# The last twelve row tiles of w2: summed straight into the result's bank, in five transfers, behind the fold

## The chip, the cores and the metric

One NeuronCore of one Trainium2 chip runs the whole program. The metric is device microseconds of that core. Before the change the median is 772.49 us over three timed runs, 772.41 to 772.53 us. The profile is one more execution of the same program, taken by the hardware profiler; its span, from the first instruction to the last, is 771.0 us.

## The reference

One decoding step of a transformer block with attention and a feed-forward part side by side, in float32, for two batch rows of 1024 numbers:

```python
xn = layernorm(x)
q = xn @ wq                                  # 32 heads of 128, 4 key/value heads
p = softmax(q k^T * 128 ** -0.5)             # over a cache of 32768 keys
o = p v
h = silu(xn @ w1)                            # 1024 -> 3584
y = x + o @ wo + h @ w2                      # wo: 4096 x 1024, w2: 3584 x 1024
```

Each weight and each cache entry is read once and used for two rows only (for eight query heads in the caches), so the work is almost all reading: 331 MB.

## The kernel before

**The stream.** SyncE issues all large transfers in one fixed order from one queue (helper `load`, L164 to L167). They fill two buffers in turn, `bufA` and `bufB`, each 128 partitions of 64 KB. A step is one filling of a buffer: wq and w1 (4 steps), the caches (32 steps, four for each pair of key/value head and batch row), wo (2 steps), w2 (2 steps). A transfer into a buffer is issued when the buffer was released: `step(n)` names the semaphore and the count for that. w2 has 28 row tiles of 128 rows. Tiles 0 to 15 (`w2a`) come into bufA in two halves, L178 and L179, and tiles 16 to 27 (`w2b`) into bufB in seven pieces, L180 to L182: six tiles, two tiles, three single tiles, and the last tile as three quarters and one quarter of its columns.

**TensorE's program.** TensorE runs a loop over pairs of steps (L321 to L347): `slots(0)` multiplies what is in bufA, `slots(1)` what is in bufB. A call works through 32 blocks of 512 columns: 16 go into each of two PSUM banks. Inside a bank the four quarters of the output partitions take four blocks side by side, and four rounds are summed into them. In the last pair, bufA holds w2a, and only the first bank's 16 blocks of bufB are worked through (`slots(1, (0,))`, tiles 16 to 23); then the branch at L327 leaves the loop. The semaphore `more[1]`, which the last pair waits for in the fourth round (two tiles of the second piece), is taken in every turn.

**The paired sums and the fold.** What such a call leaves in PSUM are paired sums: on each quarter of the partitions stands the sum over every second tile, for one half of the 1024 output columns. They are collected. ScalarE copies the two banks of wo's first step, of wo's second and of w2a into `ev[0]`, `ev[1]`, `ev[2]` (L242 to L244); GpSimd adds them and the residual `xs` (L368 to L372); VectorE adds the two halves of the sum into `rest` (L374), and then adds bufB's bank (L376) into `ob`. Two matmuls with a 0/1 matrix, the fold (L398, L399), add the quarters that belong together and put the sum into `acc`, a bank of 128 partitions x 256 columns, in which each quarter of the partitions holds 256 of the output columns.

**The direct tiles.** Tiles 24 to 27 are not paired: function `tile` (L390) multiplies one tile's four column groups of 256 straight into acc, four matmuls on the four quarters of the partitions. The order on TensorE after the loop is: tile 24, tile 25, wait for `ob` (semaphore `tob`, L397), fold, tile 26, three quarters of tile 27, the last quarter. L375 makes VectorE wait for tile 24's mark, which stands behind all of bufB's paired blocks. ScalarE then copies acc to `ot` (L246), SyncE stores it (L379), and the program ends when the store has landed (L384).

**Lines the prediction names.** L107 is the matmul helper, so all matmuls have that line; they are told apart by tile: `xy` (the paired sums' banks, `ps[0]` and `ps[1]` are its halves), `acc`, and `smA`, `smB` for the softmax. L49 is the wait in `take`, L44 the semaphore step in `pass_on`.

## Time and profile before

| what | value |
|---|---|
| timed, median of 3 | 772.49 us (772.41 to 772.53) |
| span of the profiled execution | 771.0 us |
| DMA queue, share of 16 engines | 99.5% |
| HBM read | 331.38 MB, 430 GB/s over the span |
| TensorE matmul busy | 389.6 us, 51% |
| VectorE, GpSimd, ScalarE busy | 132.3, 44.2, 28.4 us |
| mean granted TensorE clock | 0.757 |

The execution that was profiled has no time of its own beside its span. The timed runs hold 772.49 - 771.0 = about 1.5 us that lie around the span. In the prediction, times of places are microseconds from the span's start. An arrow `out<-in` gives the tensors; a shape such as `128*32 128x256` is a matmul with a 128x32 stationary operand and a 256-column output. Each float32 matmul of the program stands as two MATMUL and two LDWEIGHTS records, so `x8` is four matmuls. "idle before <-releaser" says how long an engine stood idle and what ended it.

### The profile page before, as it was taken

How to read it: one execution, taken by the hardware profiler on the slowest of the kernel's cores; microseconds unless marked ns; L12 is line 12 of the kernel's file. 1: busy time of each engine (PE TensorE's matmuls, PEld its weight loads, DVE VectorE, ACT ScalarE, POOL GpSimd, SP SyncE). 2: the span in 40 equal slices, each digit the busy share in tenths (PEclk: the TensorE clock that was granted, in tenths of full speed). 3: DMA queues.
4: the chain of work that ended last, by engine and by line, in shares of the span. 5: the costliest groups of instructions: out<-in, count | busy, mean ns of one | idle time of the engine just before them, and what ended most of it. 6: DMA issues, size and time to landing. Idle time of an engine off the chain costs nothing. (4 is left out here: it accounts for less than half of the span.)

```text
span 771.0 us, 6110 instructions
## 1 busy us (share of the span) xinstructions
PE 389.6 (51%) x2702; PEld 124.5 (16%) x2702; DVE 132.3 (17%) x98; ACT 28.4 (4%) x37; POOL 44.2 (6%) x65
## 2 busy tenths in 40 slices
PE   0454545455545454645455545444645455545466
PEld 0111211121112111211121112111211121112122
DVE  2000104030403040304030303040303030313000
ACT  0000100100010001000100010001000100010000
POOL 3001200000000100010001000100010001000121
PEclk9967677776677777677776677777677776677688
DMA  9999999999999999999999999999999999999997
GB/s 383 435 435 435 435 435 435 435 435 435 435 435 435 435 435 435 435 435 435 435 435 435 435 428 428 418 428 432 425 432 435 435 435 435 435 435 435 435 432 331
DMA packets 6944, 331.40 MB, mean 430 GB/s; under 512 B 776, under 2 KB 920, under 8 KB 1440
## 3 DMA queue, kind: packets, MB, share of 16 engines
q1 hardware_dynamic: 6928, 331.37, 99.5%
q10 hardware_dynamic: 16, 0.03, 0.0%
HBM read 331.38 MB, written 0.02 MB: 430 GB/s over the span
## 5 line engine op out<-in xcount | busy, mean ns | idle before, releaser
L107 PE MATMUL xy<-bufB,weights 128*32 128x512 f32 x1248 | 176.2, 727 | 169.3 <-PEq L49 169.3
L107 PE MATMUL xy<-bufA,weights 128*32 128x512 f32 x1280 | 180.4, 726 | 101.0 <-PEq L49 101.0
L107 PEld LDWEIGHTS xy<-bufB,weights 128*32 128x32 f32 x1248 | 48.8, 131 | 296.7 <-issue 296.5
L107 PEld LDWEIGHTS xy<-bufA,weights 128*32 128x32 f32 x1280 | 49.6, 130 | 215.5 <-issue 215.5
L258 DVE STREAM_TRANSPOSE st<-xy 128x2048 f32<-128x2048 f32 x8 | 18.5, 2316 | 243.2 <-PE xy L107 243.2
L268 DVE TENSOR_REDUCE blank<-xy 128x512 f32<-128x2048 f32 x8 | 18.3, 2292 | 222.8 <-PE xy L107 222.8
L280 POOL MEMSET weights<- 128x2048 f32 x8 | 14.4, 1804 | 525.3 <-POOLq L49 525.3
L107 PE MATMUL smA<-blank 128*8 128x128 f32 x20 | 5.4, 370 | 51.9 <-PEq L49 51.9
L259 DVE TENSOR_REDUCE blank<-st 128x8 f32<-128x2048 f32 x8 | 30.5, 3809 | 0.3
L107 PE MATMUL smA<-blank,ones 128*128 128x8 f32 x18 | 4.9, 347 | 50.6 <-PEq L49 50.6
L269 DVE TENSOR_REDUCE blank<-weights 128x8 f32<-128x2048 f32 x8 | 30.4, 3799 | 0.0
L235 ACT ACTIVATE weights<-st 128x1024 f32<-128x1024 f32 x16 | 16.0, 1048 | 328.3 <-DVE st L265 328.3
L265 DVE TENSOR_TENSOR st<-st,gmax 128x2048 f32<-128x2048 f32 x8 | 18.3, 2293 | 0.3
L107 PE MATMUL smB<-blank 128*128 128x8 f32 x72 | 15.9, 349 | 0.0
L107 PEld LDWEIGHTS smB<-blank 128*128 128x128 f32 x72 | 15.6, 317 | 0.0
L107 PEld LDWEIGHTS smA<-blank,ones 128*128 128x128 f32 x18 | 4.3, 298 | 58.5 <-issue 58.5
L238 ACT COPY blank<-onew 128x8 f32<-128x8 f32 x8 | 1.6, 204 | 277.8 <-DVE onew L272 277.8
L107 PEld LDWEIGHTS smA<-blank 128*8 128x8 f32 x20 | 1.3, 89 | 60.2 <-issue 60.2
L374 DVE TENSOR_TENSOR rest<-ev 128x512 f32<-128x512 f32 x1 | 0.7, 693 | 49.1 <-POOL ev L372 49.1
L107 PE MATMUL smB<-blank,ones 8*128 8x8 f32 x20 | 5.3, 333 | 5.7 <-PEq L49 5.7
L286 POOL COPY weights<-qall 128x128 f32 x32 | 8.0, 292 | 3.1 <-POOL weights L280 3.1
L212 DVE STREAM_TRANSPOSE tqs<-sumq 128x1024 f32<-128x1024 f32 x1 | 1.2, 1245 | 39.4 <-POOL sumq L196 39.4
(54 smaller groups left out, 57.7 us busy)
## 6 DMA issues: line engine op xcount, KB each, us to landing
bufA<-in_w2a SPq DMA_DIRECT2D x2, 4096.0 KB, 23.7
bufA<-in_w1b SPq DMA_DIRECT2D x1, 6144.0 KB, 24.6
bufB<-in_w2b SPq DMA_DIRECT2D x1, 3072.0 KB, 17.9
bufB<-in_w2b SPq DMA_DIRECT2D x3, 512.0 KB, 21.6
bufB<-in_w2b SPq DMA_DIRECT2D x1, 1024.0 KB, 20.0
bufB<-in_w2b SPq DMA_DIRECT2D x1, 384.0 KB, 23.0
bufA<-in_kt SPq DMA_DIRECT2D x8, 27.8
bufB<-in_kt SPq DMA_DIRECT2D x8, 29.2
```

The lines of the kernel that those rows point to most:

```text
L107: return T.matmul(o, lhsT, rhs, start=start, stop=stop)
L212: i_q = dve.mark(V.transpose(tqs.rearrange("p c m -> p (c m)"), sumq))
L235: A.activation(wt[c].rearrange("p e m -> p (e m)"), st[:, 1024 * c:1024 * c + 1024], AF.Exp, scale=SCALE).then_inc(tok[c], 1)
L238: A.copy(oT[:, REP * h:REP * (h + 1), 16 * b], onew).then_inc(tq, 1)
L258: then(3, V.transpose(st, xy))
L259: V.tensor_reduce(rm, e8.rearrange("p n m -> p m n"), AX.X, ALU.max).then_inc(trm, 1)
L265: V.tensor_sub(e8, e8, gmax.to_broadcast([P, 256, REP])).then_inc(subbed, 1)
L268: V.tensor_reduce(ob, xy.rearrange("p (c n) -> p n c", c=4), AX.X, ALU.add).then_inc(tob, 1)
L269: V.tensor_reduce(lsum, weights.rearrange("p e (r m) -> p m (e r)", m=REP), AX.X, ALU.add).then_inc(tls, 1)
L280: G.memset(weights, 0.0).then_inc(pself, 1)
L286: m = G.tensor_copy(o, q[:, None, None, :].to_broadcast([P, 4, 4, REP]))
L374: t = dve.mark(V.tensor_add(rest, ev[0][:, :512], ev[0][:, 512:]))
```

## The change

w2b's twelve tiles are no longer split into eight paired and four direct ones. All twelve go straight into acc. The table `PIECES` lists five transfers (first tile, end tile, first column and end column of each quarter): seven tiles, three tiles, one tile, and the last one as before in three quarters and one quarter. TensorE's loop is left after `slots(0)` of the last pair, the semaphore of bufB's second piece goes, and the fold stands first behind the loop: the wait for `tob`, the fold's two matmuls, which now open acc, and then the twelve tiles piece by piece. ScalarE no longer copies w2a's banks and GpSimd no longer adds them: VectorE adds the two banks to `rest` itself. GpSimd writes one weight block less.

```diff
+PIECES = ((0, 7, 0, QW), (7, 10, 0, QW), (10, 11, 0, QW), (11, 12, 0, CUT), (11, 12, CUT, QW))
...
-    load(0, slice(W // 2, W), w2a[:, W // 2:], more[0], 0)
-    cuts = [0, 6 * D, 8 * D, 9 * D, 10 * D, 11 * D, 11 * D + 4 * CUT, 12 * D]
-    for lo, hi, s in zip(cuts, cuts[1:], [ld[1], more[1], *last]):
-        load(1, slice(lo, hi), w2b[:, lo:hi], s, STEPS - 2 if lo == 0 else 0)
+    load(0, slice(W // 2, W), w2a[:, W // 2:], more, 0)
+    for (t0, t1, lo, hi), s in zip(PIECES, last):
+        at = slice(t0 * D + 4 * lo, (t1 - 1) * D + 4 * hi)
+        load(1, at, w2b[:, at], s, STEPS - 2 if t0 == 0 else 0)
...
-    for n in range(3):
-        act.wait(step(STEPS - 3 + n) if n < 2 else (turn_sem, 5))
-        outs.append(act.mark(A.copy(ev[n], ps[n % 2])))
-    act.wait((pe, 2))
+    for n in range(2):
+        act.wait(step(STEPS - 3 + n))
+        outs.append(act.mark(A.copy(ev[n], ps[n])))
+    act.wait((pe, 1))
...
         taken(0)
-        slots(0, (0, 1)).then_inc(turn_sem, 1)
-        taken(1)
-        slots(1, (0,))
+        slots(0).then_inc(turn_sem, 1)
         T.br_eq(pair, PAIRS - 1, on_true="te_rest", on_false="te_more")
     with nc.body("te_more", valid_engines=engine):
-        slots(1, (1,)).then_inc(turn_sem, 1)
+        taken(1)
+        slots(1).then_inc(turn_sem, 1)
...
-    for c, n in enumerate((16, 8)):
-        pool.wait(outs[c])
-        G.tensor_copy(wt[c][:, :2 * n].rearrange("p (t d) m -> p t d m", d=2),
-                      hT[:, 16 * c:16 * c + n, None, :].to_broadcast([P, n, 2, 32])).then_inc(tok[c], 1)
+    pool.wait(outs[0])
+    G.tensor_copy(wt[0].rearrange("p (t d) m -> p t d m", d=2),
+                  hT[:, :16, None, :].to_broadcast([P, 16, 2, 32])).then_inc(tok[0], 1)
+    pool.wait(outs[1])
     t = pool.mark(G.tensor_add(ev[0], ev[0], ev[1]))
     pool.wait(t)
     t = pool.mark(G.tensor_add(ev[0][:64, :512], ev[0][:64, :512], xs[:64, 256:768]))
-    pool.wait(t, outs[2])
-    t = pool.mark(G.tensor_add(ev[0], ev[0], ev[2]))
     dve.wait(t)
     t = dve.mark(V.tensor_add(rest, ev[0][:, :512], ev[0][:, 512:]))
-    dve.wait(t, (pe, 1))
-    V.tensor_add(ob, rest, ps[1][:, :512]).then_inc(tob, 1)
+    dve.wait(t, (turn_sem, 5))
+    t = dve.mark(V.tensor_add(rest, rest, ps[0][:, :512]))
+    dve.wait(t)
+    V.tensor_add(ob, rest, ps[0][:, 512:]).then_inc(tob, 1)
...
-    pe.mark(tile(0, acc, 8 * D, QW, True))
-    tile(1, acc, 9 * D, QW)
+    def tile(t, lo, hi, start=False, stop=False):
+        at = buf[1][:, t * D + 4 * lo:t * D + 4 * hi].rearrange("p (j n) -> p j n", j=4)
+        return [mm(acc[32 * j:32 * j + 32, lo:hi], hT[:, 16 + t, :], at[:, j], start, stop) for j in range(4)][-1]
+
     T.wait_ge(tob, 1)
     for c in range(2):
-        mm(acc, fold[:, 32 - 32 * c:160 - 32 * c], ob[:, c * QW:(c + 1) * QW], False, False)
-    tile(2, acc, 10 * D, QW)
-    tile(3, acc[:, :CUT], 11 * D, CUT)
-    pe.mark(tile(4, acc[:, CUT:], 11 * D + 4 * CUT, QW - CUT, False, True))
+        mm(acc, fold[:, 32 - 32 * c:160 - 32 * c], ob[:, c * QW:(c + 1) * QW], c == 0, False)
+    for (t0, t1, lo, hi), s in zip(PIECES, last):
+        T.wait_ge(s, 16)
+        for t in range(t0, t1):
+            m = tile(t, lo, hi, False, hi == QW and t == 11)
+    pe.mark(m)
```

What stands in the programs of TensorE and VectorE at the three places that matter, word for word, before (-) and after (+). Two lines more at the head of the changed file shift its numbers: L109 there is L107 here. TensorE behind the loop, from the softmax's last small matmuls (`smB`) on; `blank` holds the fold's input `ob` and hT, `bufB` holds w2b:

```order
-L107 MATMUL smB<-blank 128x8 x4
-L347 UNCONDITIONAL_BRANCH
-L107 MATMUL acc<-bufB,blank 32x256 x8
-L107 MATMUL acc<-blank 128x256 x2
-L107 MATMUL acc<-bufB,blank 32x256 x4
-L107 MATMUL acc<-bufB,blank 32x192 x4
-L107 MATMUL acc<-bufB,blank 32x64 x4
```

```order
+L109 MATMUL smB<-blank 128x8 x4
+L348 UNCONDITIONAL_BRANCH
+L109 MATMUL acc<-blank 128x256 x2
+L109 MATMUL acc<-bufB,blank 32x256 x44
+L109 MATMUL acc<-bufB,blank 32x192 x4
+L109 MATMUL acc<-bufB,blank 32x64 x4
```

The fold (128x256 x2) has moved ahead of all direct tiles, and these are 44 matmuls of full width in place of 12. TensorE's loop, from `slots(0)` to the end of the second body:

```order
-L107 MATMUL xy<-bufA,weights 32x512 x32
-L107 MATMUL xy<-bufB,weights 32x512 x16
-L327 COMPARE_AND_BRANCH
-L107 MATMUL xy<-bufB,weights 32x512 x16
-L330 REGISTER_ALU
-L331 COMPARE_AND_BRANCH
```

```order
+L109 MATMUL xy<-bufA,weights 32x512 x32
+L327 COMPARE_AND_BRANCH
+L109 MATMUL xy<-bufB,weights 32x512 x32
+L331 REGISTER_ALU
+L332 COMPARE_AND_BRANCH
```

The branch that leaves the loop now stands ahead of bufB's first block. VectorE's last instructions, from the end of its loop on:

```order
-L271 RECIPROCAL rl<-smA 128x8
-L272 TENSOR_TENSOR onew<-smB,rl 128x8
-L351 REGISTER_ALU
-L352 COMPARE_AND_BRANCH
-L374 TENSOR_TENSOR rest<-ev 128x512
-L376 TENSOR_TENSOR blank<-rest,xy 128x512
```

```order
+L352 REGISTER_ALU
+L353 COMPARE_AND_BRANCH
+L373 TENSOR_TENSOR rest<-ev 128x512
+L375 TENSOR_TENSOR rest<-rest,xy 128x512
+L377 TENSOR_TENSOR blank<-rest,xy 128x512
```

One addition has come in: w2a's two banks are read from PSUM here, one after the other.

More of the change, by code (lines that the diff above doesn't have):

```diff
@@ L70, in gqa_plus_mlp_kernel @@
     buf = [sb(n, P, W) for n in ("bufA", "bufB")]
-    ld, more, tok = ([sem(f"{n}{k}") for k in "AB"] for n in ("ld", "more", "tok"))
+    ld, tok = ([sem(f"{n}{k}") for k in "AB"] for n in ("ld", "tok"))
+    more = sem("moreA")
     ldx, turn_sem = (sem(n) for n in ("ldx", "marks"))
@@ L74, in gqa_plus_mlp_kernel @@
     trm, tgd, tls, tob = (sem(n) for n in ("trm", "tgd", "tls", "tob"))
-    last = [sem(f"last{i}") for i in range(5)]
+    last = [sem(f"last{i}") for i in range(len(PIECES))]
     done = sem("done")
@@ L288, in stage, with slots @@
         G.sem_inc(pself, -1)
-    def slots(k, banks):
+    def slots(k):
         m = None
-        for bk in banks:
+        for bk in range(2):
+            if (k, bk) == (0, 1):
+                pe.take(more, 16)
             for r in range(4):
-                if (k, bk, r) in ((0, 1, 0), (1, 0, 3)):
-                    pe.take(more[k], 16)
                 for q in range(4):
@@ L312, in gqa_plus_mlp_kernel @@
     pe.wait(i_const)
-    for s, n in ((trm, 1), (tgd, 1), (tls, 1), (tob, 1), (more[0], 16 * PAIRS - 16), (more[1], 16 * PAIRS - 16)):
+    for s, n in ((trm, 1), (tgd, 1), (tls, 1), (tob, 1), (more, 16 * PAIRS - 16)):
         T.sem_inc(s, n)
@@ L385, in gqa_plus_mlp_kernel @@
     sp.sem_inc(done, -16)
-    def quarter(o, lhsT, w, start=False, stop=False):
-        return [mm(o[32 * j:32 * j + 32, :], lhsT[j], w[j], start, stop) for j in range(4)][-1]
-    def tile(t, o, lo, n, start=False, stop=False):
-        T.wait_ge(last[t], 16)
-        at = buf[1][:, lo:lo + 4 * n].rearrange("p (j n) -> p j n", j=4)
-        return quarter(o, [hT[:, min(24 + t, FT - 1), :]] * 4, [at[:, j] for j in range(4)], start, stop)
-    pe.mark(tile(0, acc, 8 * D, QW, True))
-    tile(1, acc, 9 * D, QW)
+    def tile(t, lo, hi, start=False, stop=False):
+        at = buf[1][:, t * D + 4 * lo:t * D + 4 * hi].rearrange("p (j n) -> p j n", j=4)
+        return [mm(acc[32 * j:32 * j + 32, lo:hi], hT[:, 16 + t, :], at[:, j], start, stop) for j in range(4)][-1]
     T.wait_ge(tob, 1)
     for c in range(2):
-        mm(acc, fold[:, 32 - 32 * c:160 - 32 * c], ob[:, c * QW:(c + 1) * QW], False, False)
-    tile(2, acc, 10 * D, QW)
-    tile(3, acc[:, :CUT], 11 * D, CUT)
-    pe.mark(tile(4, acc[:, CUT:], 11 * D + 4 * CUT, QW - CUT, False, True))
+        mm(acc, fold[:, 32 - 32 * c:160 - 32 * c], ob[:, c * QW:(c + 1) * QW], c == 0, False)
[4 more added lines that the diff above has]
+    pe.mark(m)
 def kernel(A_x, A_k_cache, A_v_cache, A_wq, A_wo, B_x, B_w1, B_w2):
```

## The prediction

> **What bounds the kernel now.** I read the page first: the transfer rates by slice, the queue's share and the landing times of the large loads.

> ```profile
> GB/s 383 435 435 435 435 435 435 435 435 435 435 435 435 435 435 435 435 435 435 435 435 435 435 428 428 418 428 432 425 432 435 435 435 435 435 435 435 435 432 331
> q1 hardware_dynamic: 6928, 331.37, 99.5%
> bufA<-in_kt SPq DMA_DIRECT2D x8, 27.8
> bufB<-in_kt SPq DMA_DIRECT2D x8, 29.2
> ```

> The queue never pauses, at 435 GB/s. One buffer of 128 x 64 KB = 8.39 MB takes 8.39/435 = 19.3 us, yet a load of it lands 27.8 us after its issue: it is issued 27.8 - 19.3 = 8.5 us before the queue gets to it. So in the loop the transfers set the pace, with 8.5 us to spare before a late TensorE could make the queue run dry. Only the last slice can change. Then the chain that ended last, in order of time (start, length, what):

> ```profile
> 744.13 21.65 DMA bufB<-in_w2b
> 765.82 2.95 PE acc L107 x36
> 768.79 0.37 ACT ot L246
> ```

> Read as it stands, it says that transfers bind until tile 25 (landed 765.78) and TensorE from there: tile 25, fold, tiles 26 and 27. If that held, moving the fold would shorten the end. Whether TensorE really had no pause I take from the landings. SyncE's issues in the timeline, and the answers on transfers, one each for the first and the last four of w2b's seven pieces in order of issue (KB, us from issue to landing), with the store of the result last:

> ```profile
> 742.81 3.17 SPq L167 DMA_DIRECT2D bufB<-in_w2b  x7
> ...
> 743.65 0.91 SPq L167 DMA_DIRECT2D bufB<-in_w2b  x2
> ...
> 744.60 0.91 SPq L167 DMA_DIRECT2D bufB<-in_w2b  x2
> ...
> 769.19 0.55 SPq L379 DMA_DIRECT2D out_y<-ot  x1
> ```

> ```profile
> bufB<-in_w2b SPq DMA_DIRECT2D x1, 3072.0 KB, 17.9
> bufB<-in_w2b SPq DMA_DIRECT2D x1, 512.0 KB, 21.6
> bufB<-in_w2b SPq DMA_DIRECT2D x1, 512.0 KB, 22.5
> bufB<-in_w2b SPq DMA_DIRECT2D x1, 384.0 KB, 23.0
> bufB<-in_w2b SPq DMA_DIRECT2D x1, 128.0 KB, 22.8
> out_y<-ot SPq DMA_DIRECT2D x1, 16.0 KB, 1.8
> ```

> The issues lie about 0.47 us apart (seven in 3.17), so the first starts at 742.81 and the last four at 744.13, 744.60, 745.08 and 745.55. Those pieces land at 760.7, 765.75, 767.1, 768.1 and 768.35. Now TensorE's matmuls in the timeline, and below them its weight loads, each of which starts when its piece may be used:

> ```profile
> 753.55 5.58 PE L107 MATMUL xy<-bufA,weights 128*32 128x512 f32 x32 [5.94 <-PEq L49]
> 761.02 3.64 PE L107 MATMUL xy<-bufB,weights 128*32 128x512 f32 x32 [1.89 <-PEq L49]
> ...
> 766.39 1.13 PE L107 MATMUL acc<-blank 128*128 128x256 f32 x4
> 767.45 1.28 PE L107 MATMUL acc<-bufB,blank 128*32 128x256 f32 x24
> ```

> ```profile
> 766.39 0.73 PEld L107 LDWEIGHTS acc<-blank 128*128 128x128 f32 x4 [0.41 <-DVE blank L376]
> 767.45 0.16 PEld L107 LDWEIGHTS acc<-bufB,blank 128*32 128x32 f32 x8 [0.33 <-DMA bufB<-in_w2b]
> 768.08 0.16 PEld L107 LDWEIGHTS acc<-bufB,blank 128*32 128x32 f32 x8 [0.48 <-DMA bufB<-in_w2b]
> 768.39 0.17 PEld L107 LDWEIGHTS acc<-bufB,blank 128*32 128x32 f32 x8 [0.15 <-DMA bufB<-in_w2b]
> ```

> Tile 26 starts at 767.45, 0.35 us after its landing (767.1): there the fold was in the way. But tile 27's first part starts at 768.08 and its last at 768.39, each right at its landing (768.1 and 768.35). The delay behind the fold was made good before that. So the transfers bind to the very end, and the rest is fixed: last landing 768.35, last four matmuls until 768.77, copy 0.37, store from 769.19 and 1.8 to land, 771.0.

> **The transfers.** The bytes stay, and the last piece is the same 128 KB. From the first piece's landing (760.7) to the fourth's (765.75), 2.10 MB take 5.05 us, 415 GB/s; at 435 they would take 4.82 us, 0.23 less. The 64 KB rows of the large loads run at 435, those of 8 and 4 KB a little slower, and the change makes rows of 28 and 12 KB of them. I take 0.15 us saved; the ends are 0 (bytes unchanged) and 0.23. A price per transfer, bounded by the nearest row: the last piece, 0.131 MB, lands about 0.3 us after the one ahead of it, and at 435 GB/s its bytes alone take 0.30, so two transfers fewer save less than 0.1 us. Taken together: first new piece (3.67 MB, tiles 16 to 22) at 760.7 + 0.524/435 GB/s = 761.9, second (tiles 23 to 25) at about 765.6, tile 26 at 766.95, tile 27 at 767.95 and 768.2.

> **The road to the fold.** The edit puts the fold first, so all twelve tiles are queued on TensorE behind the wait for `tob`. These rows carry its time: VectorE's addition from PSUM, ScalarE's copy of w2a's banks, GpSimd's additions.

> ```profile
> 765.33 0.69 DVE L376 TENSOR_TENSOR blank<-rest,xy 128x512 f32<-128x512 f32 x1 [1.89 <-PE acc L107]
> ```

> ```profile
> 759.19 1.01 ACT L244 COPY ev<-xy 128x1024 f32<-128x1024 f32 x1 [15.37 <-PE xy L107]
> ```

> ```profile
> 746.92 1.26 POOL L370 TENSOR_TENSOR ev<-ev,xs 64x512 f32<-64x512 f32 x1
> 760.35 2.36 POOL L372 TENSOR_TENSOR ev<-ev 128x1024 f32<-128x1024 f32 x1 [12.17 <-ACT ev L244]
> ```

> The copy (1.01) and the addition of 2.36 us go; `rest` is ready at about 746.92 + 1.26 + 0.69 = 748.9 and waits for w2a's blocks. Those end at 753.55 + 5.58 = 759.13. Then two VectorE additions of 0.69 with some 0.1 us of signalling around each: 759.25 to 760.7. From the end of `ob` (765.33 + 0.69 = 766.02) to the fold's first load (766.39) it took 0.37, so the fold starts at 761.1, 5.3 us earlier than now. From its first load to tile 26's it took 767.45 - 766.39 = 1.06: TensorE is free for tiles at 762.15, 0.25 after the first piece. The leave of the loop ahead of bufB is hidden by that wait for VectorE.

> **The tiles.** The same matmuls on the same 3 MB; only the destination and the width change. The three-quarter tile keeps TensorE 768.39 - 768.08 = 0.31 at full clock, so a tile takes 0.31/0.75 = 0.41 to 0.43. As a cross-check, eight paired tiles in 3.64 us are 0.45 each, with the pipeline's run-out. Seven tiles: 762.15 + 3.0 = 765.15, ahead of the second piece (765.6). Three more: 765.6 + 1.3 = 766.9, ahead of tile 26 (766.95), which is done by 767.4, ahead of tile 27 (767.95). The end hangs on the last landing, 768.2, as now. Fold and twelve tiles need 1.06 + 12 x 0.43 = 6.2 us, so the fold may start as late as 768.2 - 6.2 = 762.0: 0.9 us of cover. Each us beyond it costs one.

> **What else moves.** In the loop a take of a semaphore goes and a branch moves in front of bufB's wait; both lie under the 8.5 us of lead. GpSimd's smaller weight block and SyncE's two issues fewer lie beside the stream. All of this I cost at nothing; it would take a delay of over 8.5 us on TensorE per step to show.

> **Sum.** -0.15 us (0 to -0.23): span 771.0 - 0.15 = 770.85, and 772.49 - 0.15 = 772.34 on the median. A measurement of this kernel can tell about 0.2%, 1.5 us, from no change.

> **The rivals.**

> *Faster, because TensorE's tail or the number of transfers is the price.* For it: the chain's own reading, 2.95 us of TensorE at the end. If the fold's 1.06 us lay on the path, 771.4 would come out, still within 0.2%. Against it: both parts of tile 27 start at their landings. [...] Chance of more than 0.2% faster: 3%.

> *Slower, because the clock falls in the new gap.* TensorE's windows (us, busy us, granted clock; transfers behind):

> ```profile
> 747.26:750.68 3.42, 0.35 (x4) 1.00 1.07 460
> 750.68:754.09 3.41, 0.54 (x4) 0.50 0.90 384
> 754.09:757.50 3.41, 3.41 (x20) 0.50 1.04 447
> 757.50:760.92 3.42, 1.63 (x16) 1.00 0.87 371
> 760.92:764.33 3.41, 3.31 (x32) 1.00 0.99 404
> 764.33:767.74 3.41, 2.77 (x32) 1.00 0.99 388
> ```

> After a window of 0.35 us busy the clock is halved; after one of 3.41 it is full again; 1.63 us kept it. The new gap, 759.13 to 761.1, is about the old one (1.89 us ahead of 761.02), so the same window stays at 1.63, and the next ones hold the fold and tiles, over 2.4 us each. [...] A window placed otherwise in another run could come below 1.63. One window at half: the fold takes 2.1 until 763.2, 1.3 tiles by 764.33, the other 10.7 at 0.43 end at 768.95 instead of 768.5: +0.4, 772.9, not to be told from none. Half until 767.74: fold until 763.2, 5.3 tiles at 0.85, 6.7 at 0.43 until 770.6, 2.1 us late: 774.6, 0.27% slower. It decides from there: two windows, with everything queued behind the fold. Or the same by a `tob` that comes 2.4 us later than reckoned (0.9 cover + 1.5). Against both: the windows above, and the two additions' measured 0.69. Chance 5%.

> *The transfers don't come as told.* Larger pieces land later as a whole: were the second piece's three tiles to wait until 766.5, they would end at 767.8, still ahead of tile 27. That gives 772.3 too, and belongs to the forecast.

> **How the numbers follow.** The forecast, the same end at 772.3, has 92%; faster 3%, slower 5%. The likeliest case reaches from 0.23 saved, with the timed runs' own spread of 0.12, at 772.1 to one half-clock window at 772.9. The range takes in the chain's reading half-way and some scatter between builds: 771.9 to 773.0.

> **What would show it.** Right: the fold's loads near 761.1 on a release by VectorE; the seven tiles in one run of 3.0 us; small waits for transfers ahead of tiles 23, 26 and 27; the last loads within 0.1 us of the last landing near 768.2. Wrong: a last landing more than 0.5 us from there; a granted clock of 0.5 between 760.9 and 767.7; the last loads starting well behind their landing.

## The result, and the profile after

The changed kernel takes 776.93 us (median of five runs, 776.73 to 777.57) against 772.49 us (772.41 to 772.54): a ratio of 1.0059, interval 1.0048 to 1.007. It is 0.6% slower, 4.4 us, where the prediction was no change at 772.3 us. The profiled execution has a span of 775.4 us.

The transfers first, for they are what the forecast rested on. SyncE's five issues of w2b (start, length, count), and the pieces in order of issue (KB, us from issue to landing):

```profile
744.24 2.23 SPq L169 DMA_DIRECT2D bufB<-in_w2b  x5
```

```profile
bufB<-in_w2b SPq DMA_DIRECT2D x1, 3584.0 KB, 17.7
bufB<-in_w2b SPq DMA_DIRECT2D x1, 1536.0 KB, 21.0
bufB<-in_w2b SPq DMA_DIRECT2D x1, 512.0 KB, 21.8
bufB<-in_w2b SPq DMA_DIRECT2D x1, 384.0 KB, 22.4
bufB<-in_w2b SPq DMA_DIRECT2D x1, 128.0 KB, 22.2
```

Issued at 744.24, 744.61, 745.09, 745.56 and 746.04, they land at 761.9, 765.6, 766.9, 768.0 and 768.2, each within 0.1 us of the forecast (761.9, 765.6, 766.95, 767.95, 768.2). The end no longer hangs on them. The chain that ended last:

```profile
744.61 21.01 DMA bufB<-in_w2b
765.62 0.04 issue
765.66 0.83 PE acc L109 x9
766.49 3.56 issue
770.05 3.14 PE acc L109 x36
```

"issue" is time in which TensorE waited for nothing that the profile shows. TensorE's matmuls, and below them its weight loads, from VectorE's release of the fold on:

```profile
760.48 1.13 PE L109 MATMUL acc<-blank 128*128 128x256 f32 x4 [1.61 <-DVE blank L377]
761.96 3.23 PE L109 MATMUL acc<-bufB,blank 128*32 128x256 f32 x56 [0.35 <-DMA bufB<-in_w2b]
765.66 0.83 PE L109 MATMUL acc<-bufB,blank 128*32 128x256 f32 x9 [0.47 <-DMA bufB<-in_w2b]
770.05 3.12 PE L109 MATMUL acc<-bufB,blank 128*32 128x256 f32 x39 [3.56 <-issue]
```

```profile
765.66 0.57 PEld L109 LDWEIGHTS acc<-bufB,blank 128*32 128x32 f32 x10 [0.95 <-DMA bufB<-in_w2b]
770.05 0.96 PEld L109 LDWEIGHTS acc<-bufB,blank 128*32 128x32 f32 x19 [3.83 <-issue]
```

The fold comes at 760.48 (761.1 was said) and seven tiles run through in 3.23 us (3.0 was said). Then TensorE stops in the middle of a tile: ten weight loads and nine matmul records into the second piece, all of whose data had landed. No semaphore stands between record nine and record ten. The page's part on the queues has a line that the kernel before lacks:

```profile
q1 hardware_dynamic: 6640, 331.37, 98.9%
q8 instruction: 2, 0.03, 0.0%
```

Two packets, 0.03 MB together, are on a queue that the page calls instruction; the second moves at 328 GB/s in one slice of 0.05 us, which makes it 16 KB. No such packet is moved before 767 us; the first one comes between 767 and 769 us, in the pause, the second between 771 and 773.

Behind the pause TensorE is slow as well. Its windows in stretches of 3.41 us (start and end, us, busy, granted clock, DMA share, GB/s):

```profile
760.40:763.81 3.41, 2.98 (x40) 1.00 0.85 358
763.81:767.22 3.41, 2.21 (x37) 1.00 0.98 393
767.22:770.63 3.41, 0.58 (x12) 1.00 0.10 32
770.63:774.04 3.41, 2.54 (x35) 0.50 0.02 5
```

After the window with 0.58 us of work the granted clock was 0.50; after those with 2.98 and 2.21 us it was 1.00. The 39 records that were left should take 23 x 0.43/8 for those of full width, 0.31 and 0.11 for the divided tile and 0.27 to run out (the last four matmuls of before took 768.77 - 768.39 = 0.38, of which 0.11 is the pace), 1.9 us in all; they took 3.14. So of the 4.6 us by which the last matmul is later than the last landing allowed (773.19 against 768.24 and 0.4 for the last four matmuls), about 1.2 us are the clock and the rest the pause, net of the wait for tiles 26 and 27 that it covers.

### The profile page after: what moved, and what is told of

The parts are those of the page before. It is cut to its first block, busy times and chain, and to the rows that moved or that the text cites. A ratio compares the mean times of both kernels' runs of the same rounds, so it can differ in the third digit from the quotient of the medians.

```text
span 775.4 us, 6146 instructions
## 1 busy us (share of the span) xinstructions
PE 393.7 (51%) x2734; PEld 128.4 (17%) x2734; DVE 133.0 (17%) x99; ACT 27.3 (4%) x36; POOL 41.4 (5%) x63
## 3 DMA queue, kind: packets, MB, share of 16 engines
q1 hardware_dynamic: 6640, 331.37, 98.9%
## 5 line engine op out<-in xcount | busy, mean ns | idle before, releaser
L109 PE MATMUL xy<-bufB,weights 128*32 128x512 f32 x1216 | 177.9, 750 | 164.9 <-PEq L50 164.9
L109 PE MATMUL xy<-bufA,weights 128*32 128x512 f32 x1280 | 178.0, 718 | 100.4 <-PEq L50 100.4
L109 PEld LDWEIGHTS xy<-bufB,weights 128*32 128x32 f32 x1216 | 49.0, 134 | 293.8 <-issue 293.8
L109 PEld LDWEIGHTS xy<-bufA,weights 128*32 128x32 f32 x1280 | 49.7, 129 | 212.2 <-issue 212.2
L109 PE MATMUL smA<-blank 128*8 128x128 f32 x20 | 5.4, 370 | 51.9 <-PEq L50 51.9
L109 PE MATMUL smA<-blank,ones 128*128 128x8 f32 x18 | 4.9, 347 | 50.6 <-PEq L50 50.6
L109 PE MATMUL smB<-blank 128*128 128x8 f32 x72 | 15.9, 349 | 0.0
L109 PEld LDWEIGHTS smB<-blank 128*128 128x128 f32 x72 | 15.6, 317 | 0.0
L109 PEld LDWEIGHTS smA<-blank,ones 128*128 128x128 f32 x18 | 4.3, 298 | 58.5 <-issue 58.5
L109 PEld LDWEIGHTS smA<-blank 128*8 128x8 f32 x20 | 1.3, 89 | 60.2 <-issue 60.2
L109 PE MATMUL acc<-bufB,blank 128*32 128x256 f32 (+2 forms) x104 | 7.2, 419 | 4.4 <-issue 3.6
L109 PE MATMUL smB<-blank,ones 8*128 8x8 f32 x20 | 5.3, 333 | 5.7 <-PEq L50 5.7
## 6 DMA issues: line engine op xcount, KB each, us to landing
bufB<-in_w2b SPq DMA_DIRECT2D x1, 512.0 KB, 21.8
bufB<-in_w2b SPq DMA_DIRECT2D x1, 384.0 KB, 22.4
```

What stands on the lines that cost most here:

```text
L109: return T.matmul(o, lhsT, rhs, start=start, stop=stop)
```

## The experiments

**Theory A** supposes that the pause hangs on the place in TensorE's program: that its instructions come to it in pieces such as the 16 KB packets of the instruction queue, and that the code from the tenth record on lies in a piece that is fetched only when it is reached. I call this one the third piece and the code ahead of it the first and the second. These are names: no run shows how the code ahead of it is divided. The loop's body multiplies every buffer, so the eight paired tiles of before had no code of their own. Now all twelve tiles are written out behind the loop, and the program has grown past that place, which I call the limit or the boundary. **Theory B**: the new order or the long run of direct matmuls makes TensorE pause.

I count TensorE's program so: four instructions for each float32 matmul (two weight loads, two matmuls), one for each semaphore step, branch and register step. The kernel before has 401, the changed one 527, that is 126 more: 128 for the 32 added matmuls behind the loop, less two elsewhere. The pause lies ahead of the changed kernel's 451st; the limit, then, is behind the 450th. In the experiments instructions of no effect are put ahead of the loop, where TensorE waits for the first load (until 23 us). They shift all that follows in the program and leave its instructions as they are. With 19 to 64 steps the first matmul starts at 23.1 us, as without them (23.0); with 139 it starts at 27.95. The steps are written so:

```python
    for d in [1, -1] * (n // 2):          # an odd n begins with [1, 1, -2]
        T.sem_inc(trm, d)
```

**The kernel before with 64 such steps.** By the count they put the limit behind the first weight load of the last part of tile 27. The first time in what was expected is theory A's, the other B's.

> The kernel before, with 64 semaphore steps (pairs of +1 and -1) put ahead of TensorE's loop, where TensorE waits for the first load anyway; nothing else differs. [...] The profile shows an instruction queue with 16 KB packets, TensorE stands still for 2.5 to 4 us from about 768.4, and the time is 775 to 776.5 us. Theory B (the new order or the longer run of direct matmuls costs the time): nothing changes, 772.5 us.

Measured 775.63 us, as theory A expected, ratio 1.0041, interval 1.0025 to 1.0056. Its weight loads at the end, and its page's queues:

```profile
768.35 0.16 PEld L107 LDWEIGHTS acc<-bufB,blank 128*32 128x32 f32 x8 [0.47 <-DMA bufB<-in_w2b]
768.66 0.11 PEld L107 LDWEIGHTS acc<-bufB,blank 128*32 128x32 f32 x1 [0.16 <-DMA bufB<-in_w2b]
771.78 0.15 PEld L107 LDWEIGHTS acc<-bufB,blank 128*32 128x32 f32 x7 [3.02 <-issue]
```

```profile
q8 instruction: 1, 0.02, 0.0%
```

One weight load of the last part of tile 27, then 3.02 us of nothing: the place is right to the instruction, in a kernel whose arithmetic, order and transfers are those of before. Theory B does not give this.

**Theory's limit to one instruction: 49 and 50 steps on the kernel before.** With 49 its last matmul record is the 450th counted instruction, with 50 the 451st. Theory A expects no pause ahead of it with 49, and 772.4 to 774.0 us.

> [...] Theory B (what moved the time of the kernel with 64 steps was the steps themselves, in proportion to their number): 772.47 + 49/64 x 3.16 = 774.9 us.

> One semaphore step more than the kernel beside it: the last matmul record is now the first instruction of the third piece. Theory A: TensorE pauses for about 3 us ahead of this one record, 775.3 to 775.9 us, about 3 us more than with 49. Theory B: 774.9 us, not to be told from 49 steps.

Measured 773.34 us (ratio 1.0013, interval 1.0003 to 1.0022) and 775.47 us (1.004, 1.0026 to 1.0054). TensorE's last matmuls with 49 steps:

```profile
767.52 1.28 PE L107 MATMUL acc<-bufB,blank 128*32 128x256 f32 x24
```

and with 50:

```profile
767.47 1.28 PE L107 MATMUL acc<-bufB,blank 128*32 128x256 f32 x23
771.55 0.22 PE L107 MATMUL acc<-bufB,blank 128*32 128x64 f32 x1 [2.80 <-issue]
```

With 50 steps a single record is left over and comes 2.8 us after the others. One instruction costs 2.1 us in time and 2.6 in span (771.4 to 774.0). With 49 TensorE ends at 768.8 like before. About half of the 0.9 us over 772.45 lies around the span (in the median of the runs 1.8 us of the time are outside of it, 1.4 before), the other half in it (771.55 against 771.1, medians too). One packet is fetched there too (`q8 instruction: 1, 0.02`); that it is what costs the 0.9 us is not shown apart.

**The changed kernel with the limit elsewhere: 19 and 139 steps.** With 139 the 451st counted instruction is the first behind the loop, the fold's.

> The changed kernel with 19 semaphore steps of net zero ahead of the loop, so that the boundary falls between the first piece's seven tiles and the second's three. Theory A: the pause moves from the tenth matmul record of tiles 23 to 25 to the first, it starts up to 1.3 us earlier, overlaps the wait for the second piece, and the time is 774.0 to 776.0 us. Theory B: the same place and 776.9 us.

> [...] Theory A: the fetch starts when the loop is left, near 758.4, while TensorE waits for VectorE's additions and the first piece of w2b (761.96); it is over by about 762.3, the tiles make that good, and the time is 772.2 to 772.9 us. Theory B: the pause has nothing to do with the place of the code, 776.9 us.

With 19 steps 777.61 us (ratio 1.0065, interval 1.0049 to 1.008). The pause moved, as it should, to between the seven tiles and the three:

```profile
762.11 3.23 PE L109 MATMUL acc<-bufB,blank 128*32 128x256 f32 x56 [0.72 <-DMA bufB<-in_w2b]
769.66 4.05 PE L109 MATMUL acc<-bufB,blank 128*32 128x256 f32 x48 [4.32 <-issue]
```

The time did not fall as expected: the pause grew to 4.32 us. TensorE stopped 1.15 us earlier than in the changed kernel (765.34 against 766.49), but it went on only 0.4 us earlier (769.66 against 770.05), with 48 records to go instead of 39 and at half the pace for part of them: from 770.58 to 772.71 four weight loads came in 0.43 us each time, in which the seven tiles have eight. The place is as theory A says, the length of a pause is not a constant (2.8 to 4.3 us here). With 139 steps it is 773.60 us (1.0015, 1.0006 to 1.0024): 3.3 us of the 4.4 are gone, with every matmul and transfer of the change in place. The pause now stands ahead of the fold:

```profile
761.60 1.13 PE L109 MATMUL acc<-blank 128*128 128x256 f32 x4 [3.02 <-issue]
763.20 7.03 PE L109 MATMUL acc<-bufB,blank 128*32 128x256 f32 x104 [0.47 <-DMA bufB<-in_w2b]
```

But 772.2 to 772.9 was expected. The loop's late start is not the reason: it had been made good, for VectorE's addition behind w2a's blocks starts at 758.72, 759.01 in the changed kernel. The first piece of w2b, however, landed at 763.15, 1.2 us later than the 761.9 of the changed kernel. The fetch was in the queues at that time:

```profile
q1 hardware_dynamic: 44, 1.26, 98.8%
q8 instruction: 1, 0.02, 2.2%
```

That is the window from 758 to 761 us; 2.2% of 16 engines in 3 us are 1.06 us of one. The loads behind it came about as much later, the last one at 769.55 (768.24 in the changed kernel). A smaller part is TensorE's pace: from 763.20 to 766.60 it has four weight loads in 0.43 us, behind that 68 in 3.47. The last matmul ends at 770.28, 0.3 us later than the last landing and the 0.4 us of four matmuls allow.

**The changed kernel with as little code as before.**

> The changed kernel without the matmuls of eight of the twelve tiles of w2b (only tiles 16, 23, 26 and 27 are summed; all five transfers stay), so that TensorE has as many matmuls behind the loop as before. Theory A: no instruction queue in the profile, no pause, last landing 768.2, time 772.2 to 772.5 us. Theory B, as a cost of the fold standing first or of the five transfers: the pause stays and the time is near 776.9; as a cost of the long run of direct matmuls it would fall here too, which the two kernels beside this one tell apart.

```diff
-        for t in range(t0, t1):
+        for t in (t for t in range(t0, t1) if t in (0, 7, 10, 11)):
```

Measured 772.67 us, ratio 1.0004, interval 0.9995 to 1.0013; no instruction queue on its page. It is 0.2 us above the expected range, and TensorE's pace at the end can account for that: tile 27's 16 weight loads take 0.84 us (767.94 to 768.78), where before they took 0.48 (768.08 to 768.56), and the last matmul ends at 769.07, not 768.77. Fold first, five transfers, VectorE's two additions: none of them costs time that can be told from nothing. Nor does the 0.15 us of the shorter stream show.

**The fetch kept out of the end.** In the loop the kernels write a branch hint at its head, in each turn. The question was what it does to the fetches.

> The changed kernel without the branch hint at the head of TensorE's loop. [...] If the hint does not matter for what is held: the same two packets at the end and 776 to 778 us.

```diff
-        again = T.mark_branch_hint_location()
...
-        T.br("te_loop").branch_hint(again)
+        T.br("te_loop")
```

Measured 773.62 us (1.0015, 1.0005 to 1.0026), below what a hint without effect would give, and 3.3 us faster than with the hint. There is no pause at the end:

```profile
763.42 3.23 PE L109 MATMUL acc<-bufB,blank 128*32 128x256 f32 x56
767.12 1.93 PE L109 MATMUL acc<-bufB,blank 128*32 128x256 f32 x32 [0.47 <-DMA bufB<-in_w2b]
769.36 0.64 PE L109 MATMUL acc<-bufB,blank 128*32 128x192 f32 x16 [0.31 <-DMA bufB<-in_w2b]
```

An instruction packet comes early, in the window from 44 to 50 us:

```profile
q1 hardware_dynamic: 108, 2.65, 103.6%
q8 instruction: 1, 0.02, 1.1%
```

The queues of the long stretch behind it, 50 to 760 us, have the one line of the loads:

```profile
q1 hardware_dynamic: 5554, 307.61, 100.1%
```

The page counts two packets (`q8 instruction: 2, 0.03`). The other is moved outside of 40 to 760 us; what it carries is not shown.

That the early packet is the third piece is inferred: TensorE runs through the place of the pause and waits for w2b's transfers alone (0.47 and 0.31 us). If it is, the piece was held through all the turns of the loop from 50 us on. In the changed kernel, with the hint, no packet is moved before 767 us. Between the two kernels lie the two lines of the diff and nothing else; by what way the hint does it was not shown. Tile 27's first matmul starts at 769.36, right behind its landing, which was at 768.0 in the changed kernel: the stream is 1.3 us late, and that is what remains of the cost. To have that price alone:

> The kernel before without the branch hint at the head of TensorE's loop; all else as before. [...] Theory A as the runs so far leave it (the hint keeps the third piece from being fetched ahead; a fetch holds one of the transfer queues for about 1.1 us and every later load lands that much later): one 16 KB packet near 47 us, all landings after it 1.1 to 1.4 us late, no pause at the end, 773.4 to 773.9 us. If a fetch ahead costs nothing and the 1.2 us of the changed kernel without the hint were the change's own: 772.4 to 772.6 us.

The kernel before without the hint takes 773.78 us, ratio 1.0017, interval 1.0008 to 1.0026: one packet is fetched, although its 401 counted instructions end ahead of the limit, and it ends 1.3 us later. TensorE's last stretch, to be held against 761.02, 765.82 and 767.45 of before:

```profile
762.27 3.64 PE L107 MATMUL xy<-bufB,weights 128*32 128x512 f32 x32 [2.19 <-PEq L49]
...
767.06 0.64 PE L107 MATMUL acc<-bufB,blank 128*32 128x256 f32 x8 [0.64 <-DMA bufB<-in_w2b]
...
768.69 1.23 PE L107 MATMUL acc<-bufB,blank 128*32 128x256 f32 x24
```

Everything is 1.24 us late, with one instruction packet of 0.02 MB, which starts between 46 and 49 us, as the only difference in traffic that the views show. The delay begins right there. The steps ahead of the packet and behind it, before and without the hint:

```profile
42.35 9.62 PE L107 MATMUL xy<-bufB,weights 128*32 128x512 f32 x64 [10.29 <-PEq L49]
...
56.97 7.43 PE L107 MATMUL xy<-bufA,weights 128*32 128x512 f32 x48 [4.49 <-PEq L49]
```

```profile
42.39 9.93 PE L107 MATMUL xy<-bufB,weights 128*32 128x512 f32 x64 [9.98 <-PEq L49]
...
58.22 2.79 PE L107 MATMUL xy<-bufA,weights 128*32 128x512 f32 x12 [5.39 <-PEq L49]
```

The step ahead starts at the same time, the one behind 1.25 us later, and at the end all is still 1.24 us late: a stream that is busy 99.5% of the time (the page before) has no gap in which to make that good.

**The limit inside the loop.** Here the hint stays, and 184 steps move the limit from the code behind the loop into the loop, behind the 266th of the changed kernel's counted instructions, which lies in `slots(1)`; tile 27 comes undivided (16 instructions fewer). Theory A then has the fetch early in the program and no pause at the end.

> [...] The fetch itself holds up one of the 16 transfer queues by about 1.1 us, as behind the 139 steps, so the last landing is near 769.3, the undivided tile costs 0.3 more, 773.4 to 774.0 us. If only TensorE's pause costs time and the fetch does not slow the loads: 772.5 to 772.8 us. Theory B: 776.9 us or more.

Measured 777.74 us (1.0069, 1.0052 to 1.0086), a miss that was the experiment's own. TensorE's first matmuls, with 139 steps (the kernel further up) and with 184:

```profile
27.95 9.41 PE L109 MATMUL xy<-bufA,weights 128*32 128x512 f32 x64 [27.95 <-PEq L50]
```

```profile
34.87 8.83 PE L109 MATMUL xy<-bufA,weights 128*32 128x512 f32 x64 [34.87 <-PEq L50]
```

A step takes (34.87 - 27.95)/45 = 0.15 us; without steps the matmuls start at 23.0. With 184 they start 12 us late, the next load into bufA is issued at 43.76 us (32.12 in the kernel before), and the queue runs dry near the start (69.8% busy from 36 to 43 us). The pause at the end is gone there too, but the time proves nothing. With 46 small matmuls in place of the steps:

> The earlier kernel with the loop in the second and third piece, its 184 slow semaphore steps (0.15 us each, which started the loop 12 us late) replaced by 46 small matmuls of the same 184 instructions. It keeps the hint. Theory A: one packet early in the program, no pause at the end, landings 1.1 to 1.4 us late, 0.3 us for the undivided last tile, 773.7 to 774.2 us. If the pause at the end comes from the hint or from the change's order and not from the place of the code: 776 us or more.

```diff
+    for _ in range(46):
+        mm(smA[:REP, :REP], ones[:REP, :REP], ident[:REP, :REP])
```

Measured 773.78 us (1.0016, 1.0007 to 1.0026), as expected. TensorE begins at 23.33 us, and the end has no pause:

```profile
23.33 9.46 PE L109 MATMUL xy<-bufA,weights 128*32 128x512 f32 x64 [15.37 <-PEq L50]
```

```profile
767.10 1.93 PE L109 MATMUL acc<-bufB,blank 128*32 128x256 f32 x32 [0.48 <-DMA bufB<-in_w2b]
769.57 0.64 PE L109 MATMUL acc<-bufB,blank 128*32 128x256 f32 x8 [0.54 <-DMA bufB<-in_w2b]
```

The next step, in bufB, is late (43.79, 42.36 in the changed kernel). When a packet comes is seen with the 184 steps, in the window from 36 to 43 us:

```profile
q1 hardware_dynamic: 48, 2.10, 69.8%
q8 instruction: 1, 0.02, 1.0%
```

At that time TensorE is still in `slots(0)` (34.87 to 43.70), by the count ahead of the limit. So with the limit inside the loop a packet came before the limit was reached, although the hint is there. That it is the third piece is inferred from the end without a pause.

The place of the code is thus enough to move the pause away, by two different ways and with the hint in or out. None of the versions that sum all twelve tiles directly beats the kernel before. In the three that hide or avoid the pause, 1.1 to 1.3 us above the kernel before remain. A version that stays within 450 counted instructions was not run.

## Why the prediction was wrong

**Right.** That the transfers bound the end of the kernel before; the landings to within 0.1 us; `rest` ready early (at 749.08 + 0.69 = 749.8, where 748.9 was said, and needed only at 759.0); the fold at 761.1 (760.48), the tiles' pace. The kernel with eight tiles left out shows that these steps alone give no change.

**Wrong.** The step that failed is in the part on the tiles: "The same matmuls on the same 3 MB; only the destination and the width change." The multiplications are the same, the instructions are not. Before, eight of the twelve tiles ran through the loop's own body. The change takes them out of it, and behind the loop 22 matmuls became 54, 88 instructions 216. The order of TensorE's program ahead of the prediction shows it (44 full-width rows in place of 12), and I read it as time on the array only. In its place the runs showed a pause of 3.56 us in the changed kernel, with a packet of the instruction queue in it, and some 1.2 us of halved clock behind it. "What else moves" lists a branch, a take and two issues as free and leaves the length of the program out altogether. No row of the profile before gave the price, because its 401 counted instructions end 49 ahead of the limit, and its page has no instruction queue.

The pause hit where no cover was left. I had reckoned 0.9 us of it ahead of the fold; a pause of 3 to 4 us inside w2b's second transfer has less, and the halved clock behind it adds 1.2.

**The rivals.** The slower one had the right sign at 5%, 774.6 us, and the wrong mechanism: no clock drop in the gap ahead of the fold (1.00 in the windows from 760.40 to 767.22), no late `tob`. Its clock price did come, but behind the pause (0.50 from 770.63 to 774.04). That each us beyond the cover costs one was not put to the test, for the fold came at 760.48, inside the cover. The rival's two times, 772.9 and 774.6, were added to the median before, 772.49; counted from the forecast 772.34 they are 0.15 lower.

The price of the third piece was 2.8 to 4.3 us of pause where the piece was fetched when it was reached, and 1.1 to 1.3 us of time where the pause was covered or gone. The latter fits a packet that takes its 1.06 us from a stream without a gap.

## What to carry to other kernels

## What the runs showed of the hardware

- One instruction more or less at the limit (49 and 50 steps): 773.34 against 775.47 us.
- The branch hint at the loop's head: with it the changed kernel had no instruction packet before 767 us and a pause of 3.56 us; without it one packet came between 44 and 50 us, none from 50 to 760, and there was no pause (776.93 and 773.62 us). The kernel before had no packet with the hint and one between 46 and 49 us without. With the limit inside the loop (184 steps) a packet came between 36 and 43 us in spite of the hint. By what way the hint makes the difference was not tried apart.
- One 16 KB fetch in a stream that is busy 99.5% of the time: the same matmuls behind later landings started 1.24 us late (768.69 against 767.45), about the 1.06 us that the packet behind the 139 steps occupies one of 16 engines. That the delay is this one engine's is inferred from the two numbers; the views do not part the engines. Behind the 139 steps the page counts two packets, and the landings were 1.2 us (the first piece of w2b) to 1.3 us (the last) late.
- Semaphore steps in a row took TensorE (34.87 - 27.95)/45 = 0.15 us each, and with 184 of them the first matmul started 12 us late: padding that outlasts the wait it stands in costs time itself.
- Open: why the pause is 4.3 us in one place and 2.8 in another, and how much code is held.
